# Windowed attention and a gated feed-forward layer on one core: the start of the kernel in another order

## The chip, the cores and the metric

The kernel runs on one core of a Trainium2 chip. The core has five engines with instruction streams of their own: TensorE (PE, matrix products; its weight loads are shown as PEld), VectorE (DVE), ScalarE (ACT), GpSimd (POOL) and SyncE (SP, here used only to issue DMAs). TensorE writes to PSUM (banks of 128 partitions x 512 f32); the other data lie in SBUF. DMAs can be issued by SP, ACT and POOL. Engines wait for one another by semaphores. The metric is the time of one execution on the device in microseconds (us), as a median over runs.

## The reference

Attention over 4 batches, 8 heads, 768 positions, 64 values per head, in which each position sees the first 4 positions (the sinks) and the last 128; its output, as 3072 tokens of 512 values, goes through a layer of 2048 hidden values with a gate. Cut to its core:

```python
keep = is_sink | in_window                  # pos < 4, or 0 <= row - col < 128
scores = where(keep, q @ k.T / 8, -1e9)
a = softmax(scores); x = a @ v              # all heads side by side: (3072, 512)
h = x @ w_in                                # (3072, 2048)
g = h / (1 + exp(-beta * h))
out = g @ w_out                             # (3072, 512) float32
```

All inputs are float32; the kernel works in bf16 with f32 sums.

## The kernel before, in words

**Tiles and units.** The tokens are cut into 8 tiles of 384. The attention of a tile is 4 units; a unit n is one batch, one pair of heads and one half of the sequence, 32 units in all. Units 0 to 3 give tile 0 (first halves of batch 0), units 4 to 7 tile 1 (second halves), and so on.

**What a unit does.** Its q, k and v are loaded in f32 (`load`), cast to bf16 on GpSimd (`cast`), q and k are turned on TensorE by six 128x128 transposes into one PSUM bank and copied to SBUF as `qkT` (`transpose_in`, L489 and L496; later units are turned by DMA). `scores` makes k times q for the blocks that the window touches, in two chunks (a into `s_ps`, b into `h_ps` or `s_ps`), and ScalarE takes the exponential E of each (L543). `attend` multiplies E by v with a column of ones added (`v_aug`), so that the sums come with it; for a second half the sinks come in by a product of `E_sink` and `v_sink` (L612). `normalise` divides (L632, L634), `transpose_out` turns the result and puts it in `xT`.

**Masks.** Units from ADDED = 4 on multiply E by a mask of zeros and ones on VectorE (`mask`, L554). Units below ADDED add a large negative number before the exponential: a product of the identity and `far_a` or `far_b` opens the PSUM sum (L528), 384 columns for each of two heads and two chunks.

**Sinks.** `k_sink` holds the four sink keys of a pair (L501, with the select `own_head`); `v_sink` holds the sinks' rows of v for all 16 pairs, bf16, with columns of ones. Two DMAs issued by GpSimd (L760) load and cast those rows straight into it, after VectorE has filled it with zeros.

**The feed-forward part.** For each tile and each of 16 pieces of 128 hidden values (`hidden`): four products (L671), a tanh on ScalarE (L679), the gate on VectorE (L693); `project` multiplies by w_out (L700), and the result goes out by DMA. The hidden pieces of tile 0 use two banks, `acc0` and `acc1`. The weights come in 16 pieces of 512 KB, cast on GpSimd (L456).

**Order.** The work is written down in program order, and a planner (`Prog.order`) lays it out on each engine: at each step it takes, by its own costs (`busy`, `lag`, `give`, constants for DMAs), the piece that can start first. The order on each engine is fixed in the program. Loads on SP keep their written order (`line`). `keep_busy` writes products of ones by ones into `acc1`; their results are not used, and 7 of the 21 read `k16` of unit 0 so as to stand behind its cast.

The names that the change touches: `constants` (L369), `load` (L416), `cast` (L459), `transpose_in` (L482), `scores_sink` (L507), `scores` (L521), `mask` (L545), and the opening of the program, L720 to L778.

Of the kernel before, what the change touches and what calls it, by code (L numbers as in the profile page):

```python
# [48 lines left out]
ADDED, FAR = 4, -float(1 << 20)  # L49
# [22 lines left out]
class Prog:  # L72
# [13 lines left out]
    FIRST_DMA = 1300.0  # L86
    DEPTH = 7
    LANDED, TURNED = 2000.0, 4000.0
# [70 lines left out]
    def order(self):  # L159
# [29 lines left out]
        while len(placed) < len(self.nodes):  # L189
            found = [(*b, e) for e in self.ENGINES if (b := best(e)) is not None]  # L190
            start, n, e = min(found, key=lambda f: (f[0], f[1].id))
            free[e] = start + n.busy
            if n.dma is None:
                n.done = start + n.busy + n.lag
            else:

                begin = max(dma_free[e], start + n.busy)
                others = [o for o in self.ENGINES if o != e and dma_free[o] > begin]
                dma_free[e] = begin + n.lag * (1 + len(others))
                for o in others:  # L200
                    dma_free[o] += min(n.lag, dma_free[o] - begin)
                n.done = dma_free[e] + (self.TURNED if n.dma[0][0] in "tx" else self.LANDED)
# [75 lines left out]
def bass_streamingllm_window__then__act_swish_beta_kernel(  # L278
# [50 lines left out]
    v_sink = sb("v_sink", (128, NPAIR, 2, D1), BF16)  # L329
# [32 lines left out]
    def select(out_ap, in_ap, patt, cmp, fill, base, cm, r, w):  # L362
        op("gp", lambda e: e.affine_select(out_ap, in_ap, patt, cmp, fill, base=base,
                                           channel_multiplier=cm), r=r, w=w)

    def fill(eng, ap, value, w, r=()):
        op(eng, lambda e: e.memset(ap, value), r=r, w=w)  # L367

    def constants():  # L369
# [4 lines left out]
        fill("dve", ones[:, :], 1.0, ["ones"])  # L374
# [3 lines left out]
        for z in range(4):  # L378
            fill("dve", v_aug[z][:, :, :, D:D1], 1.0, [("v_aug", z, 0), ("v_aug", z, 1)])
            fill("gp", k_sink[z][:, :], 0.0, [("k_sink", z)])  # L380
        fill("dve", v_sink[:, :, :, :], 0.0, ["v_sink"])
        fill("dve", v_sink[0:NSINK, :, 0, D:D1], 1.0, ["v_sink"], ["v_sink"])
        fill("dve", v_sink[HEAD1:HEAD1 + NSINK, :, 1, D:D1], 1.0, ["v_sink"], ["v_sink"])
# [4 lines left out]
               ["mask_b0"])  # L388
        select(two[:, :, 128:256], one, [[0, 2], [-1, 128]], ALU.is_ge, 0.0, -1, 1, ["ones"],
               ["mask_b1"])  # L390

        select(mask_a[:, 0:256], mask_b[:, 0:256], [[0, 256]], ALU.is_ge, 1.0, -NSINK, 1,
               ["mask_b0", "mask_b1"], ["mask_a"])
        select(mask_a[:, 256:TT], ones[:, 0:128], [[0, 128]], ALU.is_ge, 0.0, NSINK - 1, -1,
               ["ones"], ["mask_a1"])

        for far, m, w, names in ((far_a, mask_a, "far_a", MASK_A), (far_b, mask_b, "far_b", MASK_B)):
            op("dve", lambda e, far=far, m=m: e.tensor_scalar(far[:, :], m[:, :], -FAR, FAR, ALU.mult,
                                                              ALU.add), r=names, w=[w], **dve(300.0))
# [17 lines left out]
    def load(n, v_queue="sp"):  # L417
        b, hp, half, pb = place(n)
        t0 = half * TT
        if n < XBAR:  # L420
            for name, src in (("q", q), ("k", k)):
                s = src[b, 2 * hp:2 * hp + 2, t0:t0 + TT, :].rearrange("h (p c) d -> p h (c d)", c=3)
                d = stage[name][pb][:, :, 3 * half:3 * half + 3, :].rearrange("p h c d -> p h (c d)")
                op("sp", lambda e, d=d, s=s: e.dma_start(d, s),
                   w=[(name + "_stage", pb, half, 0), (name + "_stage", pb, half, 1)],
                   dma=f"{name}{pb}_{half}", line=True, **transfer(2 * TT * D * 4, 300))
        for name, src in (("q", q), ("k", k), ("v", v)):
            if name != "v" and n < XBAR:
                continue
            for hh in range(2):  # L430
                s = src[b, 2 * hp + hh, t0:t0 + TT, :].rearrange("(c p) d -> p c d", p=128)
                op(v_queue, lambda e, hh=hh, s=s, name=name: e.dma_start(
                    stage[name][pb][:, hh, 3 * half:3 * half + 3, :], s),
                   w=[(name + "_stage", pb, half, hh)], dma=f"{name}{pb}_{half}{hh}",
                   line=v_queue == "sp", **transfer(TT * D * 4, 230))
# [23 lines left out]
    def cast(n):  # L459
# [6 lines left out]
        for x, name in enumerate("qk"):  # L466
            op("gp", lambda e, x=x, name=name: e.tensor_copy(qk16[z][:, x, :, :, :], view(name)),  # L467
               r=[(name + "_stage", pb, half, hh) for hh in range(2)], w=[(name + "16", z)],
               busy=451.0, lag=100.0)
# [3 lines left out]
        if n >= XBAR:  # L473
            op("sp", lambda e: e.dma_start_transpose(
                qkT[pb][:, half, :, :].rearrange("p w (c x) -> p (w c) x", c=3),
                qk16[z][:, :, :, :, :].rearrange("p w c h d -> p (w c h d)")),
               r=[("q16", z), ("k16", z)], w=[("qkT", pb, half)], dma=f"t{pb}{half}",
               **transfer(2 * TT * 256, 240, 1400.0))


    def transpose_in(n, bank=tr_ps, name_of="tr", eng="dve"):
        _, _, half, pb = place(n)  # L482
        bank16 = bank[:, :].bitcast(BF16)
        z = n % NQK
        for which, name in enumerate("qk"):
            with P.together("pe"):
                for c in range(3):
                    at = (3 * which + c) * 128
                    op("pe", lambda e, which=which, c=c, at=at: nc.tensor.transpose(  # L489
                        bank16[:, at:at + 128],  # L490
                        qk16[z][:, which, c, :, :].rearrange("p h d -> p (h d)"), ident[:, :]),
                       r=[(name + "16", z), "ident"], w=[name_of], **pe(128))

        dst = qkT[pb][:, half, :, :].rearrange("x w (p c) -> x w p c", c=3)
        src = bank16[:, 0:2 * TT].rearrange("x (w c p) -> x w p c", w=2, c=3)
        op(eng, lambda e: (e.copy if eng == "act" else e.tensor_copy)(dst, src),  # L496
           x=[name_of], w=[("qkT", pb, half)], **(act(768) if eng == "act" else dve(865.0)))
# [9 lines left out]
    def scores_sink(n, bank, name):  # L507
# [3 lines left out]
           r=[("k_sink", pb), ("qkT", pb, 1)], w=[f"{name}0"], **pe(TT))  # L511
# [7 lines left out]
    def scores(n, c, bank, name):  # L519
# [11 lines left out]
        with P.together("pe"):  # L531
            for kb, qb, nq in CHUNKS[half][c]:
                w = 128 * nq
                for hh in range(2):
# [5 lines left out]
                       r=[("qkT", pb, half), ("qkT", pb, kb // 3)], w=[f"{name}{hh}"],  # L540
# [6 lines left out]
    def mask(n, c):  # L547
        if n < ADDED:
# [8 lines left out]
           r=[("E", n % 2, c), *names], w=[("E", n % 2, c)], **dve(466.0))  # L557

    def scores_at_once(n):
# [8 lines left out]
        with P.together("pe"):  # L568
            for x, kb, qb, nq in pieces:
                for hh in range(2):  # L570
# [6 lines left out]
                       r=[("qkT", pb, half), ("qkT", pb, kb // 3)], w=[("s0", "s1", "tr", "av")[bank]],  # L577
# [143 lines left out]
    for n in range(4):  # L721
        load(n, "act" if n < 2 else "sp")
    op("act", lambda e: e.dma_start(beta_stage[:, :], moe_beta.rearrange("(m p) -> m p", p=128)),
       w=["beta_stage"], dma="beta")
    load_w(0)
# [11 lines left out]
    cast(0)  # L737
    cast(1)

    def keep_busy(count, busy, behind=()):  # L740

        for _ in range(count):
            op("pe", lambda e: e.matmul(acc[1][:, 0:256], ones[:, 0:128], ones[:, :], start=True,  # L743
                                        stop=True), r=["ones", *behind], w=["acc1"], busy=busy,
               lag=260.0, give=200.0)
# [4 lines left out]
    def enter(n):  # L750
        transpose_in(n, *((tr_ps, "tr") if n % 2 == 0 else (acc[0], "acc0")), "dve")
        if n + 2 < 6:
            cast(n + 2)
        if n == 1:
            for i in range(4):
                cast_w(i)
            for hh in range(2):
                rows = slice(HEAD1 * hh, HEAD1 * hh + NSINK)
                s = v[:, :, 0:NSINK, :].rearrange("b (g h) s d -> s h (b g) d", h=2)[:, hh]
                op("gp", lambda e, hh=hh, rows=rows, s=s: e.dma_start(v_sink[rows, :, hh, 0:D], s),  # L760
                   w=[("v_sink", hh)], r=["v_sink"], dma=f"s{hh}")

    for n in range(4):
        enter(n)
        if n == 2:
            for hh in range(2):
                select(own_head[:, hh, :], ones[:, 0:NSINK], [[0, NSINK]], ALU.is_ge, 0.0, 63 - 127 * hh,
                       2 * hh - 1, ["ones"], ["own_head"])
        if n == 0:
            keep_busy(7, 200.0, [("k16", 0)])  # L770
# [18 lines left out]
    for n in range(4):  # L789
        sink_keys(n)  # L790
# [132 lines left out]
```

## Time and profile before

| what | us |
|---|---|
| median of 3 runs | 232.91 (232.72 to 233.29) |
| the profiled execution | 232.34 |
| its span | 230.6 |
| busy: PE, DVE, ACT, POOL | 219.8, 135.3, 138.7, 75.3 |
| first exponential starts | 10.05 |

The page divides the span into 40 slices of 5.77 us and gives the busy share in tenths. A row of the order of time has start, length, engine, line, operation, output and inputs, count, and in brackets the idle time before it with what ended it. In the chain of waits each piece is work that the end of the execution hung on. A transfer's time to landing counts from its issue. The granted clock in the windows is 1.00 throughout, though the early products take longer than the later ones of the same shape.

### The profile page before, as it was taken

What the parts mean: (1) busy time and instruction counts of PE and PEld (TensorE: products, weight loads), DVE (VectorE), ACT (ScalarE), POOL (GpSimd) and SP (SyncE); (2) the same over time, 40 slices, a digit from 0 to 9 for tenths busy, and PEclk for the clock granted to TensorE, in tenths of its full rate; (3) what the DMA queues carried; (4) which work ended last, traced back from release to release, by engine and by line L of the source; (5) the groups of instructions that cost most, each with busy time, mean ns of one, the idle gap of its engine ahead of it and who ended that gap; (6) DMA issues with size and microseconds to landing.
All of it is one profiled execution on the core that took longest, in us unless ns stands there. A gap on an engine that the chain in (4) does not pass through costs nothing.

```text
span 230.6 us, 4381 instructions
## 1 busy us (share of the span) xinstructions
PE 219.8 (95%) x1714; PEld 119.1 (52%) x1714; DVE 135.3 (59%) x261; ACT 138.7 (60%) x217; POOL 75.3 (33%) x152
## 2 busy tenths in 40 slices
PE   4997989899999999999999999999999999999994
PEld 2654545555455555545555555555555555555441
DVE  5364999699654654544577676566656554344300
ACT  2275886597418676645777776756766764555421
POOL 7769985797440331541202342500000000000000
PEclk9999999999999999999999999999999999999999
DMA  6999999996699996984999897631101101111012
GB/s 154 317 386 288 329 339 257 382 330 158 147 220 288 179 260 149 223 219 113 238 240 186 189 235 186 155 73 55 55 20 63 63 20 63 45 48 45 33 58 91
DMA packets 95700, 39.76 MB, mean 172 GB/s; under 512 B 82352, under 2 KB 88512, under 8 KB 95680
## 3 DMA queue, kind: packets, MB, share of 16 engines
q1 hardware_dynamic: 93504, 39.07, 64.6%
q10 hardware_dynamic: 1632, 0.40, 0.8%
q8 instruction: 13, 0.21, 0.3%
q0 software_dynamic: 544, 0.02, 0.2%
q14 instruction: 7, 0.06, 0.1%
HBM read 27.30 MB, written 6.29 MB: 146 GB/s over the span
## 4 chain that ended last, share of the span: by engine, by line
PE 84%; DVE 10%; ACT 4%; issue 1%; ACTq 0%
PE acc L700 35%; PE h_ps L671 28%; PE s_ps L623 5%; PE s_ps L573 4%; DVE g L693 4%; PE acc L671 3%; DVE E L554 3%; ACT E L543 2%; PE h_ps L700 2%; DVE qkT L496 2%; PE acc L743 1%; PE s_ps L536 1%; ACT th L679 1%; PE s_ps L489 1%; PE s_ps L612 1%; DVE v_sink L367 1%
## 5 line engine op out<-in xcount | busy, mean ns | idle before, releaser
L700 PE MATMUL acc<-w_out,g 128*128 128x512 bf16 x368 | 99.0, 380 | 0.0
L679 ACT ACTIVATE th<-h_ps,beta_half 128x384 f32<-128x384 f32 x104 | 59.5, 582 | 45.9 <-PE h_ps L671 43.8
L671 PE MATMUL h_ps<-xT,w_in 128*128 128x384 bf16 x416 | 80.7, 326 | 0.0
L693 DVE SCALAR_TENSOR_TENSOR g<-th,h_ps 128x384 bf16<-128x384 f32 x104 | 56.4, 551 | 38.2 <-ACT th L679 36.8
L671 PEld LDWEIGHTS h_ps<-xT,w_in 128*128 128x128 bf16 x416 | 39.9, 98 | 32.6 <-DVE g L693 1.4
L700 PEld LDWEIGHTS acc<-w_out,g 128*128 128x128 bf16 x368 | 33.8, 98 | 31.7 <-issue 3.0
L589 DVE TENSOR_TENSOR E<-E,mask_all 128x1536 bf16<-128x1536 bf16 x20 | 19.5, 975 | 20.2 <-ACT E L580 20.2
L580 ACT ACTIVATE E<-s_ps 128x1536 bf16<-128x1536 f32 x20 | 28.9, 1445 | 2.0 <-PE s_ps L573 1.9
L470 POOL CAST v_aug<-v_stage 128x384 bf16<-128x384 f32 x32 | 16.6, 527 | 28.1 <-DMA v_stage<-in_v_dram 14.9
L467 POOL CAST qk<-q_stage 128x384 bf16<-128x384 f32 x32 | 18.0, 562 | 23.7 <-DMA q_stage<-in_q_dram 10.8
L467 POOL CAST qk<-k_stage 128x384 bf16<-128x384 f32 x32 | 17.1, 535 | 15.2 <-DMA k_stage<-in_k_dram 13.8
L708 ACT ACTIVATE out_sb<-acc 128x512 f32<-128x512 f32 x23 | 13.6, 597 | 14.1 <-PE acc L700 13.7
L671 PE MATMUL acc<-xT,w_in 128*128 128x384 bf16 x96 | 19.0, 327 | 2.4 <-DVE g L693 1.8
L543 ACT ACTIVATE E<-s_ps 128x768 bf16<-128x768 f32 x16 | 13.0, 811 | 13.5 <-PE s_ps L536 13.5
L623 PEld LDWEIGHTS s_ps<-v_aug,E 128*128 128x128 bf16 x384 | 17.1, 97 | 5.5 <-ACT E L543 0.7
L623 PE MATMUL s_ps<-v_aug,E 128*128 128x65 bf16 x384 | 19.4, 193 | 0.5 <-ACT E L543 0.4
L634 DVE TENSOR_TENSOR o_norm<-s_ps,rden 128x384 bf16<-128x384 f32 x32 | 17.8, 557 | 1.5
L679 ACT ACTIVATE th<-acc,beta_half 128x384 f32<-128x384 f32 x24 | 13.7, 581 | 5.9 <-PE acc L671 5.2
L693 DVE SCALAR_TENSOR_TENSOR g<-th,acc 128x384 bf16<-128x384 f32 x24 | 12.8, 545 | 3.8 <-ACT th L679 3.7
L496 DVE COPY qkT<-s_ps 128x768 bf16<-128x768 bf16 x10 | 9.5, 954 | 5.5 <-PE s_ps L489 5.4
L671 PEld LDWEIGHTS acc<-xT,w_in 128*128 128x128 bf16 x96 | 8.2, 98 | 8.3 <-DVE g L693 3.2
L573 PE MATMUL s_ps<-qkT 64*128 64x256 bf16 (+2 forms) x144 | 10.1, 254 | 0.0
(65 smaller groups left out, 148.4 us busy)
## 6 DMA issues: line engine op xcount, KB each, us to landing
out_dram<-out_sb SPq DMA_DIRECT2D x24, 256.0 KB, 2.3
wst<-in_moe_w_in_dram SPq DMA_DIRECT2D x8, 512.0 KB, 5.3
wst<-in_moe_w_out_dram SPq DMA_DIRECT2D x8, 512.0 KB, 8.9
q_stage<-in_q_dram SPq DMA_DIRECT2D x8, 384.0 KB, 4.3
k_stage<-in_k_dram SPq DMA_DIRECT2D x8, 384.0 KB, 4.2
v_stage<-in_v_dram SPq DMA_DIRECT2D x8, 384.0 KB, 3.9
v_stage<-in_v_dram SPq DMA_DIRECT2D x28, 96.0 KB, 4.8
q_stage<-in_q_dram SPq DMA_DIRECT2D x12, 192.0 KB, 5.3
```

Of the source, the lines that this page charges most:

```text
L467: op("gp", lambda e, x=x, name=name: e.tensor_copy(qk16[z][:, x, :, :, :], view(name)), r=[(name + "_stage", pb, half, hh) for hh in range ...
L470: op("gp", lambda e: e.tensor_copy(v_aug[pb][:, 3 * half:3 * half + 3, :, 0:D], view("v")), r=[("v_stage", pb, half, hh) for hh in range(2 ...
L543: op("act", lambda e: e.activation(E[n % 2][:, c, :, 0:at], bank[:, 0:2, 0:at], AF.Exp, bias=0.0, scale=SCALE), x=[f"{name}0", f"{name}1"] ...
L573: op("pe", lambda e, kb=kb, bank=bank, qb=qb, at=at, nq=nq, rows=rows: e.matmul(s_ps[:, bank, 128 * at:128 * (at + nq)], qkT[pb][rows, kb ...
L580: op("act", lambda e: e.activation(E[z][:, :, :, :].rearrange("p c h x -> p c (h x)"), s_ps[:, :, :].rearrange("p (h b) x -> p h (b x)", h ...
L589: op("dve", lambda e: e.tensor_tensor(both, both, mask_all[:, half, :].unsqueeze(1).to_broadcast([128, 2, 768]), ALU.mult), r=[("E", z, 0) ...
L623: last=(x == len(kbs) - 1): e.matmul(av_ps[:, at + hh * D1:at + hh * D1 + D1], E[z][:, c, h2, col:col + 128], v_aug[pb][:, kb, hh, :], sta ...
L634: op("dve", lambda e: e.tensor_tensor(o_norm[o][:, :, :, :].rearrange("p m h d -> p (m h) d"), src[:, :, 0:D], rden[z][:, :].unsqueeze(2). ...
L671: return op("pe", lambda e: e.matmul(bank, w_in16[:, c, m * 128:(m + 1) * 128], xT[:, c, T * TT:(T + 1) * TT], start=(c == 0), stop=(c == 3)),
L679: op("act", lambda e: e.activation(th[i % 3][:, :], bank, AF.Tanh, bias=0.0, scale=beta_half[:, m:m + 1]), x=[name], r=["beta"], w=[("th", ...
L693: op("dve", lambda e: e.scalar_tensor_tensor(g[T % 2][:, m, :], th[i % 3][:, :], 1.0, bank, ALU.add, ALU.mult), r=[("th", i % 3)], x=[name ...
L700: node = op("pe", lambda e: e.matmul(bank, g[T % 2][:, m, t * 128:(t + 1) * 128], w_out16[:, m, :], start=(m == 0), stop=(m == NM - 1)), r ...
```

## The change

1. *Loads.* Of units 0 and 1, q goes by SP and k by ScalarE's queue, and of v one head by each, behind q and k of both units. Before, q and k went by SP and v by ScalarE. From unit 2 on the loads stand as before.
2. *Casts of unit 0.* k is cast on VectorE, q on GpSimd.
3. *Transposes of unit 0.* q goes into `s_ps`, copied by VectorE, k into `acc0`, copied by ScalarE. The readiness of q's half (`qT`) and of all (`qkT`) is told apart.
4. *Sinks.* `own_head` moves to `sink_constants` with the fills of `k_sink` and `v_sink`; `v_sink` is filled as 1040 f32 in place of 2080 bf16 values. The sinks' rows of v go by two plain f32 DMAs on ScalarE's queue into a part of `g[1]` (not in use yet), and VectorE casts them into `v_sink` in two copies.
5. *Masks.* ADDED is 6, so units 4 and 5 get their masks by products on TensorE.
6. *Keep-busy products.* 14, then 3 behind the transposes of unit 0, then 2 behind the attention of each of units 0, 1 and 2; none reads a cast.
7. *Order.* The transposes of unit n + 1 are written ahead of unit n's attention; `sink_keys` of units 0 to 3 stands behind the attention of unit 3; several of the planner's costs have other values.

```diff
-ADDED, FAR = 4, -float(1 << 20)
+ADDED, FAR = 6, -float(1 << 20)
...
-    FIRST_DMA = 1300.0
+    FIRST_DMA = 0.0
...
+    def sink_constants():
+        for z in range(4):
+            fill("gp", k_sink[z][:, :], 0.0, [("k_sink", z)], busy=150.0)
+        for hh in range(2):
+            select(own_head[:, hh, :], ones[:, 0:NSINK], [[0, NSINK]], ALU.is_ge, 0.0, 63 - 127 * hh,
+                   2 * hh - 1, ["ones"], ["own_head"], 150.0)
+        fill("dve", v_sink_all[:, :].bitcast(F32), 0.0, ["v_sink"], busy=1000.0)
...
-    def cast(n):
+    def cast(n, first=False):
...
+            eng = "dve" if first and name == "k" else "gp"
...
-    def transpose_in(n, bank=tr_ps, name_of="tr", eng="dve"):
+    def transpose_in(n, bank=tr_ps, name_of="tr", eng="dve", apart=None):
...
+        if apart is None:
+            copy(eng, 0, 2, bank, name_of, [("qT", pb, half), ("qkT", pb, half)])
+        else:
+            copy(eng, 0, 1, bank, name_of, [("qT", pb, half)])
+            copy(apart[2], 1, 2, apart[0], apart[1], [("qkT", pb, half)])
...
-    for n in range(4):
-        load(n, "act" if n < 2 else "sp")
+    for n in range(2):
+        load_qk(n, "q")
+        load_qk(n, "k", "act")
+    for n in range(2):
+        load_head(n, "v", 0)
+        load_head(n, "v", 1, "act")
+    load(2)
+    load(3)
...
+        op("act", lambda e, rows=rows, s=s: e.dma_start(v_rows[rows], s), w=[("v_rows", hh)],
+           dma=f"s{hh}", **transfer(1 << 14, 100))
...
+        op("dve", lambda e, hh=hh, rows=rows: e.tensor_copy(v_sink[rows, :, hh, 0:D], v_rows[rows]),
+           r=[("v_rows", hh), "v_sink"], w=[("v_sink", hh), *wide], give=3000.0, **dve(600.0))
...
-                op("gp", lambda e, hh=hh, rows=rows, s=s: e.dma_start(v_sink[rows, :, hh, 0:D], s),
-                   w=[("v_sink", hh)], r=["v_sink"], dma=f"s{hh}")
...
+    turned = enter(0)
+    keep_busy(3, 200.0, turned)
     for n in range(4):
-        enter(n)
...
-        if n == 0:
-            keep_busy(7, 200.0, [("k16", 0)])
         scores(n, 0, s_ps, "s")
         scores(n, 1, h_ps, "h")
         mask(n, 0)
         mask(n, 1)
-        attend(n)
+        if n < 3:
+            enter(n + 1)
+        ended = attend(n)
         normalise(n)
         if n < 3:
             transpose_out(n, acc[1], "acc1", "act")
+            keep_busy(2, 200.0, ended)
...
-        sink_keys(n)
+        sink_keys(n, ended)
```

More of the change, by code (lines that the diff above doesn't have):

```diff
@@ L201, in order @@
                     dma_free[o] += min(n.lag, dma_free[o] - begin)
-                n.done = dma_free[e] + (self.TURNED if n.dma[0][0] in "tx" else self.LANDED)
+                n.done = dma_free[e] + (self.TURNED if n.dma[0][0] in "tx" else
+                                        self.LANDED if start > 3000.0 else self.FIRST_LANDED)
                 landing[e].append(n.done)
@@ L373, in constants @@
            r=["ones32"], w=["scratch"])
-        fill("dve", ones[:, :], 1.0, ["ones"])
+        fill("dve", ones[:, :], 1.0, ["ones"], busy=270.0)
         select(ident[:, :], ones[:, 0:128], [[1, 128]], ALU.is_equal, 0.0, 0, -1, ["ones"], ["ident"])
@@ L378, in constants @@
         for z in range(4):
[L379 to L383, printed above, removed]
+            fill("dve", v_aug[z][:, :, :, D:D1], 1.0, [("v_aug", z, 0), ("v_aug", z, 1)], busy=60.0)
         two = mask_b[:, :].rearrange("p (r x) -> p r x", r=2)
@@ L415, in load_whole, with load_qk @@
            dma=f"{name}{pb}_00", line=True, after=after, **transfer(4 * TT * D * 4, 217, 600.0))
-    def load(n, v_queue="sp"):
+    def load_qk(n, name, queue="sp"):
         b, hp, half, pb = place(n)
[L419 to L427, printed above, removed]
-            if name != "v" and n < XBAR:
[L429 to L435, printed above, removed]
@@ L539, in scores @@
                         stop=True, skip_group_check=n < ADDED),
[L540 removed]
+                       r=[("qT", pb, half), ("qkT", pb, kb // 3)], w=[f"{name}{hh}"],
                        busy=50.0 + w / 4.8, lag=260.0)
@@ L736, in bass_streamingllm_window__then__act_swish_beta_kernel, with keep_busy @@
     load_w(7)
-    cast(0)
+    cast(0, True)
     cast(1)
-    def keep_busy(count, busy, behind=()):
+    sink_constants()
+    for hh in range(2):
+        rows = slice(HEAD1 * hh, HEAD1 * hh + NSINK)
+        op("dve", lambda e, hh=hh, rows=rows: e.tensor_copy(v_sink[rows, :, hh, 0:D], v_rows[rows]),
+           r=[("v_rows", hh), "v_sink"], w=[("v_sink", hh), *wide], give=3000.0, **dve(600.0))
+    def keep_busy(count, busy, after=None):
         for _ in range(count):
             op("pe", lambda e: e.matmul(acc[1][:, 0:256], ones[:, 0:128], ones[:, :], start=True,
-                                        stop=True), r=["ones", *behind], w=["acc1"], busy=busy,
-               lag=260.0, give=200.0)
+                                        stop=True), r=["ones"], w=["acc1"], busy=busy,
+               lag=260.0, give=200.0, after=after)
     keep_busy(14, 215.0)
     def enter(n):
-        transpose_in(n, *((tr_ps, "tr") if n % 2 == 0 else (acc[0], "acc0")), "dve")
+        if n == 0:
+            turned = transpose_in(n, tr_ps, "tr", "dve", (acc[0], "acc0", "act"))
+        else:
+            turned = transpose_in(n, *((tr_ps, "tr") if n % 2 == 0 else (acc[0], "acc0")), "dve")
         if n + 2 < 6:
@@ L756, in enter @@
                 cast_w(i)
[L757 to L760, printed above, removed]
-                   w=[("v_sink", hh)], r=["v_sink"], dma=f"s{hh}")
-    for n in range(4):
-        enter(n)
[L765 to L768, printed above, removed]
-        if n == 0:
-            keep_busy(7, 200.0, [("k16", 0)])
+        return turned
+    turned = enter(0)
+    keep_busy(3, 200.0, turned)
+    for n in range(4):
         scores(n, 0, s_ps, "s")
```

80 lines of the change are left out of this document (56 added, 24 removed).

## The prediction

> **What bounds the kernel now.** I read the page first (shares, then the 40 slices), then the chain of waits, then the order of time of the first 30 us on all engines, and last the transfers' times to landing.
>
> ```profile
> span 230.6 us, 4381 instructions
> ...
> PE   4997989899999999999999999999999999999994
> ...
> DMA  6999999996699996984999897631101101111012
> ```
>
> A slice is 5.77 us. TensorE is at 9 from the ninth slice on, so whatever ends earlier in the first eight slices should end the kernel earlier by as much. The transfers are at 6 to 9 in nearly the same slices, so the start is also a race with the DMA. In order of time, the first unit's way to its first exponential (E), the later E, and unit 3's copy before the first hidden products:
>
> ```profile
> 0.81 0.45 SPq L424 DMA_DIRECT2D q_stage<-in_q_dram  x1
> ...
> 1.32 0.45 SPq L424 DMA_DIRECT2D k_stage<-in_k_dram  x1
> ...
> 1.81 2.15 DVE L367 MEMSET v_sink<- 128x2080 bf16 x3 [0.36 <-issue]
> ...
> 3.17 0.29 POOL L363 TENSOR_SCALAR_AFFINE_SELECT mask_a<-ones 128x128 bf16<-128x128 bf16 x1
> ...
> 4.21 0.25 DVE L398 TENSOR_SCALAR far_a<-mask_a 128x384 bf16<-128x384 bf16 x1
> 4.28 1.43 POOL L760 DMA_DIRECT2D v_sink<-in_v_dram  x2 [0.82 <-DVE v_sink L367]
> ...
> 6.00 0.50 POOL L467 CAST qk<-q_stage 128x384 bf16<-128x384 f32 x1
> ...
> 6.90 0.50 POOL L467 CAST qk<-k_stage 128x384 bf16<-128x384 f32 x1
> ...
> 7.74 0.85 PE L489 MATMUL s_ps<-ident,qk 128*128 128x128 bf16 x6
> ...
> 8.62 0.96 DVE L496 COPY qkT<-s_ps 128x768 bf16<-128x768 bf16 x1 [4.16 <-PE s_ps L489]
> ...
> 10.05 0.81 ACT L543 ACTIVATE E<-s_ps 128x768 bf16<-128x768 f32 x1 [7.24 <-PE s_ps L536]
> ...
> 13.23 0.96 DVE L496 COPY qkT<-s_ps 128x768 bf16<-128x768 bf16 x1
> ...
> 13.93 0.51 POOL L467 CAST qk<-k_stage 128x384 bf16<-128x384 f32 x1 [1.31 <-PE acc L743]
> ...
> 14.63 0.81 ACT L543 ACTIVATE E<-s_ps 128x768 bf16<-128x768 f32 x1 [0.16 <-PE s_ps L536]
> ...
> 17.00 0.81 ACT L543 ACTIVATE E<-s_ps 128x768 bf16<-128x768 f32 x1 [0.48 <-PE s_ps L536]
> ```
>
> GpSimd is free of masks at 3.46 but issues the sinks' two DMAs until 5.71, because these wait for VectorE's v_sink fill; only at 6.00 does it cast unit 0's q. When that had landed:
>
> ```profile
> L424 SPq DMA_DIRECT2D q_stage<-in_q_dram x1: 452/452/452, 0.8 to 0.8; - x1
> ...
> DMA to landing us min/median/max: 3.0/3.0/3.0
> L424 SPq DMA_DIRECT2D k_stage<-in_k_dram x1: 450/450/450, 1.3 to 1.3; - x1
> ...
> DMA to landing us min/median/max: 3.2/3.2/3.2
> ```
>
> q at 3.8, k at 4.5: both lay in SBUF for over 2 us. Behind unit 3, the chain of waits goes on so:
>
> ```profile
> 20.27 0.49 ACT xT L655
> 20.76 0.05 issue
> 20.81 0.35 PE acc L671
> ...
> 25.32 0.72 DVE E L554
> ...
> 26.50 0.78 DVE E L554
> ...
> 27.75 0.76 DVE E L554
> ```
>
> Hidden products of tile 0 close at 20.81. From about 24 to 38 the chain lies mostly on VectorE, and three of the four mask multiplies of units 4 and 5 are pieces of it, 2.26 us together.
>
> **The change part by part.**
>
> *Unit 0.* GpSimd loses the 1.43 us of DMA issue and the 0.82 us wait in front. It takes one of the two own_head selects ahead and can cast q at the landing, 3.8 to 4.1 (k now starts at 0.81 on ScalarE's queue beside q, where k started 0.51 later). The k cast goes to VectorE: between far_a's 0.25 and GpSimd's 0.50, I take 0.4. VectorE must be free: the v_sink fill writes 1040 f32 in place of 2080 bf16; between the 2.15 unchanged and half of it, I take half, so far_b and far_a end near 3.8 rather than 4.46. Both casts are then done by 4.7. Transposes run at the early rate, six in 0.85 with the last one's latency, to 5.5. The copy of 768 columns in 0.96 becomes two of 384, one on VectorE (half of 0.96) and one on ScalarE (0.49 by the xT piece), in two banks: done by 6.0. Before, copy end to first E was 0.47 (9.58 to 10.05). So first E at about 6.4, a gain of 3.6.
>
> *Units 1 to 3.* All four transfers of units 0 and 1's q and k go ahead of v, so unit 1 is fed by about 5.5. The period of a unit, 14.63 to 17.00, is 2.4 us, made of two E, products and a normalisation; it stays. New on VectorE are two v_sink casts (1024 elements on 4 partitions), queued before the copies of unit 2 and unit 3, and they wait for their DMAs. By far_a's rate one costs 0.66, by the copy's 1.28; I take 1.0 as the source is f32. The DMAs replace GpSimd's cast DMAs and are issued last on ScalarE's queue, at about 3.5 to 4.4; the transfer ahead of them there was beta, whose time was
>
> ```profile
> L723 ACTq DMA_DIRECT2D beta_stage<-in_moe_beta_dram x1: 505/505/505, 3.0 to 3.0; - x1
> ...
> DMA to landing us min/median/max: 5.4/5.4/5.4
> ```
>
> so they land by about 9.8. VectorE gets there at about 9.3. The first costs 0.5 of wait and 1.0 of cast before unit 2's copy, which so starts at about 10.8 where it started at 13.23. Behind that wait stand unit 2's copy, rden and o_norm; E of unit 2 waits for them. Of the 3.6, some 0.7 goes there. GpSimd's 1.31 wait at 13.93 (keep-busy products that read unit 0's k) goes; what is late next there is unit 3's q and k, which have to land by 12. Unit 3's first E comes at about 14.1 for 17.00, its xT copy at 17.4 for 20.27, hidden products close at 17.9 for 20.81: a gain of 2.9. Transposes stand now between the scores and attention of the unit before, which only moves them. The added keep-busy products are issued into waits; without that cover two cost about 0.2.
>
> *Units 4 and 5.* Four multiplies leave VectorE (2.26 on the chain). Eight products of 384 columns come to TensorE. The same product of units 0 to 3 gives their price:
>
> ```profile
> 10.92 0.50 PE L528 MATMUL s_ps<-far_a,ident 128*128 128x384 bf16 x2 [0.25 <-ACT E L543]
> ...
> 11.25 0.33 PE L489 MATMUL s_ps<-ident,qk 128*128 128x128 bf16 x3
> ```
>
> Two hold it for 0.33, eight for 1.3; the cover is TensorE's waiting in the same stretch, seen in the windows:
>
> ```profile
> 14.00:16.00 2.00, 2.00 (x30) 1.17 (x26) 1.33 (x4) 1.84 (x3) 2.00 (x4) 1.00 1.04 391
> ...
> 20.00:22.00 2.00, 1.07 (x11) 0.59 (x10) 0.20 (x1) 1.30 (x3) 2.00 (x6) 1.00 1.01 255
> ```
>
> (window, length, busy of PE, PEld, DVE, ACT, POOL, clock, DMA share, GB/s). At most the 1.3 shows, at least nothing.
>
> *The DMA's wall.* The order of SP's queue from unit 2 on is untouched, so later landings hold still.
>
> ```profile
> k_stage<-in_k_dram SPq DMA_DIRECT2D x1, 192.0 KB, 7.5
> ```
>
> (size, and us from issue to landing) and in order of time
>
> ```profile
> 10.93 0.57 SPq L424 DMA_DIRECT2D k_stage<-in_k_dram  x1
> ...
> 22.84 1.04 POOL L456 CAST w_in<-wst 128x1024 bf16<-128x1024 f32 x1 [0.33 <-DMA wst<-in_moe_w_in_dram]
> ...
> 25.63 0.77 POOL L467 CAST qk<-k_stage 128x384 bf16<-128x384 f32 x1
> ...
> 28.57 0.50 PE L489 MATMUL s_ps<-ident,qk 128*128 128x128 bf16 x6
> ```
>
> Unit 4's k lands at 18.4. The w_in piece at 22.84 and unit 6's k at 25.63 follow their landings, so they stay; unit 6's transposes began at 28.57, 2.2 after that cast ended (26.40). That is the slack: up to there about 2.2 can be gained, whatever the front and the masks give.
>
> *Sum.* Front 2.9, masks 2.26 off, products up to 1.3 on: 2.9 + 2.3 - 1.3 = 3.9 if the DMA lets it, 2.2 by the wall at unit 6. I take 2.3, as the wall holds one unit and a little comes back from casts that no longer run beside a mask multiply (0.77 for 0.50). From tile 1 on the same work is left. The profiled execution took 232.34, its span 230.6, so 1.74 lie around it; new span 228.3, execution 230.0. The median of the runs stands 0.57 above the profiled one (232.91), so 230.6.
>
> **The rivals.** *More comes through* (3.9): the wall passes over unit 6 because its place in TensorE's order is behind other ready work. For it: 2.26 on VectorE's chain. Time 229.0. Against: unit 6 is also in the chain of the first tile, whose products have two banks.
>
> *The transfers take it all:* DMA at 9 and waits for w_in; if the transfers of units 4 to 6 come later by more k ahead of v, the 2.2 of slack shrinks to about 0.4. Against: the bytes ahead of unit 4 are the same. Time 232.5.
>
> *Slower, by TensorE's clock.* Early products run at half rate:
>
> ```profile
> 5.81 2.13 PE acc L743 x10
> ```
>
> 0.213 for 256 columns, where the 384 at 10.92 take 0.165, that is 0.11 for 256. If the new order, with waits between a few products from 5 to 14, does not reach the fast rate before unit 3, each unit pays for it: TensorE is busy 2.00 of 2.00 at 14 to 16, some of it latency, so I take half of the period, 1.2, for three units: 3.6 more, 234.2. It decides from two slow units on (2.4 against the gain of 2.3). Against it: the window at 20 to 22 has only 1.07 us of busy TensorE, and the products behind it run at the full rate (28.57: six transposes in 0.50, which took 0.85 at 7.74), so short waits alone do not bring the slow rate back. I give it 0.09. The Trainium skill's page "TensorE: Matmul & The Clock Gate" (Part 1: The HAM clock gate) states that the array starts at half rate, is released after about 3.4 us of sustained work and falls back after an idle window of that length; its Part 4 (PE-mode transpose) adds that transposes do not count as busy in the same way. Read strictly, that speaks against a start with few plain products, and the time by it would be this rival's, where by the rows it is the likeliest one's.
>
> **How the numbers follow.** Likeliest, 230.6: 0.66. More, 229.0: 0.13. Transfers, 232.5: 0.12, of which 0.10 within what a measurement of this kernel tells from no change, about 0.3% or 0.7 us. Slower: 0.09. So faster 0.66 + 0.13 + 0.02 = 0.81, same 0.10, slower 0.09. The likeliest one's own range is 229.6 to 231.8 (casts of 0.66 to 1.28, and none to 1.3 of the products). The range for 8 in 10 takes in the second and most of the third: 228.8 to 233.0, with the slower case left out.
>
> **What would show it.** Right: unit 0's first E near 6.4, unit 3's near 14, the close of the first hidden products near 17.9, VectorE's L554 multiplies of units 4 and 5 gone, unit 6's transposes near 26.4, tile 1 earlier by about 2.3 and the last slices alike. Wrong: VectorE idle before a v_sink cast until past 11; half-rate products past 10; unit 6's k cast later than 25.7; or the gain at 18 there but given back by 40, which would say that the first tile is bound by something else than VectorE.

## The result and the profile after

| | before | changed |
|---|---|---|
| median of 5 runs, us | 232.91 (232.72 to 233.37) | 229.99 (229.84 to 230.45) |
| the profiled execution, its span | 232.34, 230.6 | 230.45, 228.7 |

The ratio is 0.9873, with a 95% interval of 0.9857 to 0.9889: 2.9 us faster, 0.6 below the forecast of 230.6. The profiled execution of the changed kernel is the slowest of its five, 0.46 above their median; a second one, in the experiments below, took 229.70 with a span of 228.0. All ratios here are of undisturbed executions: seven of the twelve of one run below, the kernel before with half of w_in, took 5 to 6 us longer at a lower clock and are left out.

The page of the changed kernel, the span and the slices of TensorE and of the DMA:

```profile
span 228.7 us, 4395 instructions
...
PE   7988988999999999999999999999999999999994
...
DMA  6999999998689999996999998601101201111112
```

From the eighth slice on TensorE is at 9 (before, from the ninth on), and the last slices are alike. What has gone lies in the slices ahead of that. The changed kernel in order of time, unit 0's way to its first E, the two new casts, then unit 3's E and its copy (columns as before):

```profile
3.93 0.50 POOL L481 CAST qk<-q_stage 128x384 bf16<-128x384 f32 x1 [0.25 <-DMA q_stage<-in_q_dram]
4.13 0.55 DVE L481 CAST qk<-k_stage 128x384 bf16<-128x384 f32 x1 [0.49 <-DMA k_stage<-in_k_dram]
...
5.04 0.53 PE L504 MATMUL acc<-ident,qk 128*128 128x128 bf16 x3
5.28 0.56 DVE L513 COPY qkT<-s_ps 128x384 bf16<-128x384 bf16 x1 [0.60 <-PE s_ps L504]
...
6.68 0.81 ACT L567 ACTIVATE E<-s_ps 128x768 bf16<-128x768 f32 x1 [0.60 <-PE s_ps L560]
6.89 0.51 PE L504 MATMUL acc<-ident,qk 128*128 128x128 bf16 x6
...
9.43 0.76 DVE L780 CAST v_sink<-g 4x1024 bf16<-4x1024 f32 x1
...
11.87 0.69 DVE L780 CAST v_sink<-g 4x1024 bf16<-4x1024 f32 x1
...
14.30 0.81 ACT L567 ACTIVATE E<-s_ps 128x768 bf16<-128x768 f32 x1 [0.77 <-PE s_ps L560]
...
17.58 0.48 ACT L679 COPY xT<-s_ps 128x384 bf16<-128x384 bf16 x1 [0.26 <-PE s_ps L675]
```

q and k of unit 0 are cast at their landing (3.93 and 4.13 in place of 6.00 and 6.90), and the first E starts at 6.68 for 10.05. The v_sink casts have no idle time in front, so nothing waited for the sinks' rows. Unit 3's first E comes 2.70 earlier. Then, on GpSimd and TensorE, the entry of unit 4 and of unit 6:

```profile
18.25 1.04 POOL L469 CAST w_in<-wst 128x1024 bf16<-128x1024 f32 x1 [1.58 <-DMA wst<-in_moe_w_in_dram]
...
19.22 0.51 POOL L481 CAST qk<-q_stage 128x384 bf16<-128x384 f32 x1
...
19.79 0.34 PE L504 MATMUL s_ps<-ident,qk 128*128 128x128 bf16 x3 [0.47 <-POOL qk L481]
...
26.18 0.51 POOL L481 CAST qk<-k_stage 128x384 bf16<-128x384 f32 x1
...
26.93 0.33 PE L504 MATMUL s_ps<-ident,qk 128*128 128x128 bf16 x3
```

GpSimd idles 1.58 for a piece of w_in. Unit 4's casts stand behind that piece, and TensorE waits 0.47 for the cast of its q, which ends at 19.73. Before, unit 4's six transposes began at 21.14, behind the hidden products that close at 20.81; the gain of 2.70 at unit 3's E is 1.35 at unit 4's transposes. The wait is less than what is lost; the other part is worked out below.

### The profile page after: what moved, and what is told of

The parts are those of the page before. It is cut to its first block, busy times and chain, and to the rows that moved or that the text cites. A ratio compares the mean times of both kernels' runs of the same rounds, so it can differ in the third digit from the quotient of the medians.

```text
span 228.7 us, 4395 instructions
## 1 busy us (share of the span) xinstructions
PE 220.6 (96%) x1724; PEld 119.5 (52%) x1724; DVE 134.6 (59%) x260; ACT 139.1 (61%) x218; POOL 73.3 (32%) x149
## 4 chain that ended last, share of the span: by engine, by line
PE 85%; DVE 4%; DMA 4%; SPq 4%; ACT 1%; POOL 1%; issue 1%; ACTq 0%
PE acc L724 36%; PE h_ps L695 30%; PE acc L695 4%; PE s_ps L647 4%; PE s_ps L597 4%; DMA wst<-in_moe_w_in_dram 4%; SPq L438 2%; PE h_ps L724 2%; PE s_ps L504 1%; DVE E L578 1%; DVE g L717 1%; SPq L430 1%; PE s_ps L560 1%; PE s_ps L636 1%; PE s_ps L533 1%; DVE qkT L513 1%
## 5 line engine op out<-in xcount | busy, mean ns | idle before, releaser
L481 POOL CAST qk<-q_stage 128x384 bf16<-128x384 f32 x32 | 17.3, 542 | 24.8 <-DMA q_stage<-in_q_dram 10.3
L481 POOL CAST qk<-k_stage 128x384 bf16<-128x384 f32 x31 | 16.1, 521 | 16.1 <-DMA k_stage<-in_k_dram 16.1
L513 DVE COPY qkT<-s_ps 128x768 bf16<-128x768 bf16 (+1 forms) x10 | 9.1, 914 | 1.8 <-PE s_ps L504 1.8
```

What stands on the lines that cost most here:

```text
L481: op(eng, lambda e, x=x, name=name: e.tensor_copy(qk16[z][:, x, :, :, :], view(name)), r=[(name + "_stage", pb, half, hh) for hh in range( ...
```

## The experiments

Each comparison has the kernel before beside it on the same chip (medians 232.57, 232.45 and 232.56 in three groups). Marks of the profiled executions, in us from the start of the span; "T4" is the first of unit 4's transposes on TensorE, "w_in cast" the start of that on GpSimd just ahead of unit 4's casts (no entry where three such casts run on end), "last xT copy" the start of the copy that the last products of hidden pieces 0 and 1 need:

| kernel | first E | unit 3's E | last xT copy | w_in cast | T4 | span | span - T4 |
|---|---|---|---|---|---|---|---|
| before | 10.05 | 17.00 | 20.27 | | 21.14 | 230.6 | 209.5 |
| changed, first profile | 6.68 | 14.30 | 17.58 | 18.25 | 19.79 | 228.7 | 208.9 |
| changed again (x1) | 6.13 | 13.75 | 17.02 | 17.43 | 18.97 | 228.0 | 209.0 |
| masks back (x2) | 6.37 | 13.98 | 17.26 | 16.87 | 18.83 | 228.0 | 209.2 |
| masks only (x5) | 10.02 | 16.97 | 20.24 | | 21.11 | 229.9 | 208.8 |
| sinks by GpSimd (x6) | 6.22 | 14.05 | 17.32 | 18.03 | 19.57 | 228.2 | 208.6 |
| changed, half of w_in (x8) | 6.04 | 14.96 | 18.23 | 16.02 | 19.81 | 228.4 | 208.6 |
| one bank in unit 0 (x9) | 6.78 | 14.41 | 17.82 | 16.71 | 18.76 | 227.9 | 209.1 |
| no products between (x10) | 6.08 | 13.74 | 17.40 | 16.84 | 18.39 | 227.5 | 209.1 |

From unit 3's E to the last copy of tile 0's xT it takes 3.27 or 3.28 before and in the changed kernel, so what is lost of the front's gain is lost between this copy and T4: 0.87 before, 2.21 and 1.95 in the two profiles of the changed kernel, 1.57 with the masks back. The rows of the kernel before, then those of x2:

```profile
18.85 1.14 PE L671 MATMUL acc<-xT,w_in 128*128 128x384 bf16 x6
...
20.81 0.50 PE L671 MATMUL acc<-xT,w_in 128*128 128x384 bf16 x2 [0.57 <-ACT xT L655]
...
21.14 0.50 PE L489 MATMUL s_ps<-ident,qk 128*128 128x128 bf16 x6
```

```profile
16.87 1.04 POOL L469 CAST w_in<-wst 128x1024 bf16<-128x1024 f32 x1 [0.65 <-DMA wst<-in_moe_w_in_dram]
...
17.79 0.10 PEld L695 LDWEIGHTS acc<-xT,w_in 128*128 128x128 bf16 x1 [0.47 <-ACT xT L679]
17.85 0.51 POOL L481 CAST qk<-q_stage 128x384 bf16<-128x384 f32 x1
...
17.96 0.38 PE L786 MATMUL acc<-ones 128*128 128x256 bf16 x2
...
18.18 0.81 PE L695 MATMUL acc<-xT,w_in 128*128 128x384 bf16 x4
...
18.83 0.33 PE L504 MATMUL s_ps<-ident,qk 128*128 128x128 bf16 x3
```

In both, the eight products of hidden pieces 0 and 1 stand ahead of T4. Before, six of them come ahead of the last xT copy and two wait for it. In the changed kernel and in x2 three come ahead, and five wait, with two keep-busy products among them (17.96): three products of 0.165 and two of 0.11 more, 0.7. In x2 and x8 this is the whole loss, for there the cast of unit 4's q ends before TensorE gets to T4 (18.36 against 18.83 in x2). In the two profiles of the changed kernel the late cast adds 0.64 and 0.38 (0.47 and 0.21 of idle time in the rows, which count the last product's latency as busy). In x9 and x10 six products come ahead again, and from the copy to T4 it takes 0.94 and 0.99, though the copy itself comes 0.1 and 0.4 later behind unit 3's E. This is read off the rows; no run changes that order alone.

**The masks: the changed kernel again, with them back, and alone on the kernel before.** The second and third have one edit:

```diff
-ADDED, FAR = 6, -float(1 << 20)
+ADDED, FAR = 4, -float(1 << 20)
```

> The changed kernel once more, for a second profile beside the other runs. The first profile puts the close of the first hidden products 2.7 us earlier than before (18.1 for 20.8), but hidden piece 14 only 0.5 us earlier (40.2 for 40.7), and the first products with w_out 2.1 us earlier (53.8 for 55.8). Theory T (the prediction's: front and masks give it, the order of the tail is neutral) expects 230.0 within 0.3 and, if the late transfers of the first profile are one execution's chance, piece 14 near 38.5. Theory R (the gain of the front is lost by 40 us in every execution, and the rest comes from the tail's other order) expects the same 230.0, with piece 14 again at 40 to 40.4.

> The changed kernel with the masks of units 4 and 5 back on VectorE (ADDED = 4); the order on the engines is the changed kernel's but for these instructions. Theory T: VectorE gets 2.3 us of its chain back and TensorE loses 1.3 us of products, the DMA's wall takes part of the difference, so 230.5 to 231.3, 231.0 likeliest. The rival, that the first tile is bound by transfers alone, expects 230.0 within 0.3.

> The kernel before with the masks of units 4 and 5 on TensorE (ADDED = 6), nothing else written differently. The prediction's sum gives 2.3 us off VectorE's chain and up to 1.3 on TensorE, so 1.0 faster than before, 231.6 to 231.9. The rival, after the run with the masks put back cost nothing: 0 within 0.5, because what the multiplies hold up waits for transfers or for TensorE anyway.

Measured: the changed kernel again 230.09 (ratio 0.9903, interval 0.9877 to 0.9929), masks back 230.06 (0.9900, 0.9874 to 0.9926), masks alone on the kernel before (ADDED 6 for 4) 231.73 (0.9964, 0.9952 to 0.9977). So the masks give 0.7 alone and nothing that can be measured on top of the new start; by span minus T4 it is 0.7 and 0.2. The expectation for the repeat took the hidden piece at 40.18 in the first profile for the wrong counterpart: counted through, it is piece 15, which the kernel before ran at 42.02, so 1.8 of the gain were still there at 40 us. The theory that the gain was lost by then (R) came from that miscount. Masks back lies below the 230.5 to 231.3 that was expected, within its rival's range.

**The order of the rest.** The changed kernel with every engine's order of the kernel before from hidden piece 14 on, and the reverse:

```diff
+CUT = 317
...
         placed = self.order()
+        rank = {lab: x for x, lab in enumerate(TAIL)}
+        placed[CUT:] = sorted(placed[CUT:], key=lambda n: rank["%d%s%d" % (n.lab[0], n.lab[1][0], n.lab[2])])
```

> The changed kernel up to hidden piece 14, and from there the order on every engine of the kernel before (same instructions, same waits by data). Theory T: 230.0 within 0.3, the order of the tail is neutral. Theory R: what the first profile shows between 40 and 54 us, 1.6 us of the gain (2.1 less 0.5), goes, 231.3 to 231.9.

> The kernel before up to hidden piece 14, and from there the order on every engine of the changed kernel. Theory T: 232.9 within 0.3. Theory R: 1.0 to 1.6 us faster than before, 231.3 to 231.9.

Measured: 230.54 (0.9922, 0.9898 to 0.9947) and 231.94 (0.9981, 0.9962 to 0.9999). Both point the same way, 0.45 lost and 0.6 gained with the planner's new order of the rest, but the first interval overlaps that of the changed kernel and the second just misses 1. About 0.5, not settled.

**The sinks' rows back on GpSimd,** as two casting DMAs straight into v_sink:

```diff
-        op("act", lambda e, rows=rows, s=s: e.dma_start(v_rows[rows], s), w=[("v_rows", hh)],
-           dma=f"s{hh}", **transfer(1 << 14, 100))
...
-        op("dve", lambda e, hh=hh, rows=rows: e.tensor_copy(v_sink[rows, :, hh, 0:D], v_rows[rows]),
-           r=[("v_rows", hh), "v_sink"], w=[("v_sink", hh), *wide], give=3000.0, **dve(600.0))
...
+                op("gp", lambda e, hh=hh, rows=rows, s=s: e.dma_start(v_sink[rows, :, hh, 0:D], s),
+                   w=[("v_sink", hh)], r=["v_sink"], dma=f"s{hh}")
```

> The changed kernel with the sinks' rows of v fetched again by GpSimd's two casting DMAs straight into v_sink, and without the two plain DMAs and VectorE's two casts. Theory T: the planner puts these DMAs behind the casts of unit 2 or 3 or before unit 0's; 1.4 us of GpSimd come back somewhere in the first 12 us. If ahead of unit 0's cast: first E 1.4 to 2 us later and the time 231.0 to 232.0. If behind the first units' casts: little is lost and the 1.4 us of VectorE's casts are won, 229.6 to 230.4.

Measured: 229.99 (0.9896, 0.9876 to 0.9915). In order of time:

```profile
3.93 0.50 POOL L481 CAST qk<-q_stage 128x384 bf16<-128x384 f32 x1 [0.22 <-DMA q_stage<-in_q_dram]
...
4.53 1.44 POOL L794 DMA_DIRECT2D v_sink<-in_v_dram  x2
...
6.22 0.81 ACT L567 ACTIVATE E<-s_ps 128x768 bf16<-128x768 f32 x1 [0.44 <-PE s_ps L560]
...
14.05 0.81 ACT L567 ACTIVATE E<-s_ps 128x768 bf16<-128x768 f32 x1 [0.76 <-PE s_ps L560]
```

The issue still costs GpSimd 1.44, now behind unit 0's q cast, and the first E keeps its place. So the gain of unit 0 came from what stands ahead of its cast, not from taking the DMAs away from GpSimd. Without the two casts on VectorE it still takes 7.83 from the first E to unit 3's (7.62 with them, 6.95 before): they aren't what stretches the front.

**The transfers.** Both kernels with half of each w_in piece loaded, and that half cast twice, so the hidden values are others than the reference's:

```diff
         view, src, _ = w_piece(i)
+        if i < NW:
+            view, src = view[:, :, 0:256], src[:, :, 0:256]
```

> The kernel before with half of each w_in piece loaded (256 of 512 columns, cast twice; the hidden values of the other columns are wrong), so 2 MB fewer in the first 31 us at the same instructions on all engines. Theory T (the transfers bind the first tile only once the front is early): 232.6 to 232.9, at most 0.3 faster, since before GpSimd waited 0.3 to 0.5 us at each of four pieces. Rival (transfers bind both): 1 us or more faster.

> The changed kernel with half of each w_in piece loaded in the same way (the hidden values of the other columns are wrong). Theory T: the DMA's wall took part of the 3.2 us of the front and all that the masks gave; without it the changed kernel gains 0.8 to 1.6 us more, 228.5 to 229.3. Rival (the first tile is bound by its two banks and the engines, not by transfers): 230.0 within 0.3.

Measured: the kernel before 0.9973 (0.995 to 0.9996), about 0.6 less, between the two expectations (at most 0.3, or 1 and more), so that it decides neither; the changed one 229.86 (0.9892, 0.987 to 0.9913), as with all of w_in. Its order of time, and that of the changed kernel again below it:

```profile
9.13 0.72 DVE L785 CAST v_sink<-g 4x1024 bf16<-4x1024 f32 x1
9.25 0.96 POOL L486 CAST qk<-k_stage 128x384 bf16<-128x384 f32 x1
...
11.97 2.48 POOL L474 CAST w_in<-wst 128x1024 bf16<-128x1024 f32 x2
...
12.33 1.22 DVE L785 CAST v_sink<-g 4x1024 bf16<-4x1024 f32 x1
...
17.00 0.51 POOL L486 CAST qk<-q_stage 128x384 bf16<-128x384 f32 x1
...
19.81 0.33 PE L509 MATMUL s_ps<-ident,qk 128*128 128x128 bf16 x3
...
22.80 0.51 POOL L486 CAST qk<-k_stage 128x384 bf16<-128x384 f32 x1
...
23.30 0.81 PE L700 MATMUL acc<-xT,w_in 128*128 128x384 bf16 x4
...
27.35 0.33 PE L509 MATMUL s_ps<-ident,qk 128*128 128x128 bf16 x3
```

```profile
17.43 1.04 POOL L469 CAST w_in<-wst 128x1024 bf16<-128x1024 f32 x1 [1.19 <-DMA wst<-in_moe_w_in_dram]
...
18.41 0.51 POOL L481 CAST qk<-q_stage 128x384 bf16<-128x384 f32 x1
...
18.97 0.34 PE L504 MATMUL s_ps<-ident,qk 128*128 128x128 bf16 x3 [0.21 <-POOL qk L481]
...
22.09 0.81 PE L695 MATMUL acc<-xT,w_in 128*128 128x384 bf16 x4
...
25.16 0.51 POOL L481 CAST qk<-k_stage 128x384 bf16<-128x384 f32 x1
...
26.14 0.33 PE L504 MATMUL s_ps<-ident,qk 128*128 128x128 bf16 x3
```

Two readings. At unit 6 the transfers do not bind: its k is cast 2.4 earlier with half of w_in, yet its transposes follow hidden piece 4 by 4.05 in both (23.30 to 27.35, 22.09 to 26.14). At unit 4 they do in the full kernel (the cast of q ends at 18.92, and TensorE follows at once) and not in the other one, where TensorE comes 2.3 after that cast has ended. That this did not show in the time goes with the same rows: GpSimd's casts ran beside VectorE's v_sink casts, both took longer (1.22 for 0.67 in x1, 0.96 for 0.51, two w_in casts in 2.48 for 2.03), and unit 3's E came 1.2 later. That these are all of the 1.2 is not shown. The median alone would have said that the transfers don't matter; the test took one wait away and put other delays in its place.

**Unit 0 in one bank,** k cast on GpSimd, one copy of 768 columns; tail order held:

```diff
-    cast(0, True)
+    cast(0)
...
-            turned = transpose_in(n, tr_ps, "tr", "dve", (acc[0], "acc0", "act"))
+            turned = transpose_in(n, tr_ps, "tr", "dve")
```

> The changed kernel with unit 0 as before in one respect: k cast on GpSimd behind q, all six transposes in one bank, one copy of 768 columns on VectorE. From hidden piece 14 on every engine's order is the changed kernel's. The prediction's steps: the k cast ends some 0.3 later, the copy 0.46 later (0.96 for 0.50), so unit 0's first E some 0.8 later (6.9 to 7.3); the units' period is untouched, so unit 3's first E and the end move as much: 230.8. Rival: the front's end is set by the cast of w_in that follows its landing at 17.4, and the 0.8 vanishes: 230.0 within 0.3.

Measured: 230.16 (0.9897, 0.9869 to 0.9924), so no loss. In order of time:

```profile
6.78 0.81 ACT L646 ACTIVATE E<-s_ps 128x768 bf16<-128x768 f32 x1 [3.95 <-PE s_ps L639]
...
8.45 0.81 ACT L646 ACTIVATE E<-s_ps 128x768 bf16<-128x768 f32 x1 [0.16 <-PE s_ps L639]
...
14.41 0.81 ACT L646 ACTIVATE E<-s_ps 128x768 bf16<-128x768 f32 x1 [0.49 <-PE s_ps L639]
...
18.20 0.51 POOL L560 CAST qk<-q_stage 128x384 bf16<-128x384 f32 x1 [0.45 <-DMA q_stage<-in_q_dram]
...
18.35 0.50 PE L774 MATMUL acc<-xT,w_in 128*128 128x384 bf16 x2 [0.57 <-ACT xT L758]
...
18.76 0.34 PE L583 MATMUL s_ps<-ident,qk 128*128 128x128 bf16 x3
```

The first E is 0.65 later, near the 0.8 expected. Unit 1's is where it was (8.46 in x1), but the planner has a part in that: in x1 unit 1's scores stand on TensorE behind unit 0's attention and start at 8.08, here they stand ahead of it and start at 8.07. Unit 3's E is 0.66 later again, and T4 is 0.21 earlier. Two things end together there: the cast of unit 4's q, which waited for its landing, at 18.71, and the last two hidden products, which wait for xT, at 18.68 (18.35 and twice 0.165). T4 can be early because only two hidden products stand behind the xT copy here; in x1 there are five. So the rival has the time right, but the cast of w_in that it names isn't what T4 waits for here, and as the edit brought another order on TensorE with it, the run doesn't show what the split would be worth at the end by itself.

**No keep-busy products between the units:**

```diff
-    keep_busy(3, 200.0, turned)
...
-            keep_busy(2, 200.0, ended)
```

> The changed kernel without the seven added keep-busy products that stand between the units' transposes and their first hidden products (the three behind unit 0's transposes stay, taken from the fourteen at the start); tail order as in the changed kernel. The prediction's step (they are issued into waits and cost nothing, and short waits don't bring the slow rate back): 230.0, or up to 0.3 less; six transposes stay at about 0.5. Rival, TensorE's clock: without them the products of units 1 to 3 fall back to half rate (384 columns x2 in 0.6 and more where they take 0.33), and the time is 231 to 234.

The edit takes out nine products (three, and two behind each of three units), not seven; the fourteen of the start are left.

Measured: 229.29 (229.01 to 230.16; 0.9874, 0.9842 to 0.9907), the lowest of all and below both expectations, 0.6 and 0.9 below ADDED 8 and the one-bank kernel of the same group; the ranges overlap. Three transposes among the attention of unit 2, and the first hidden products (16.82 in x1):

```profile
11.15 0.34 PE L583 MATMUL acc<-ident,qk 128*128 128x128 bf16 x3
...
15.98 1.14 PE L774 MATMUL acc<-xT,w_in 128*128 128x384 bf16 x6
```

At 0.34 for three the full rate holds without them. Whether the 0.6 is theirs stays open. Unit 3's E is where it was, and T4 comes 0.58 earlier than in x1 by two things at once: the w_in piece was cast 0.59 earlier in this execution, and six hidden products stand ahead of the last xT copy in place of three.

**More masks on TensorE,** ADDED 8 and ADDED 12:

```diff
-ADDED, FAR = 6, -float(1 << 20)
+ADDED, FAR = 8, -float(1 << 20)
```

> The changed kernel with the masks of units 6 and 7 on TensorE as well (ADDED 8): four multiplies of 0.54 to 1.2 less on VectorE, eight products of 0.165 more on TensorE. Theory V, that VectorE back to back from 29 to 37 us binds units 6 and 7 in the changed kernel: 229.2 (0.8 less, as the masks of units 4 and 5 were worth 0.8 alone). Rival P, that TensorE is as full there: 230.0 to 230.8. The tail's order comes out another way, worth 0.5 to either side.

> The changed kernel with the masks of units 6 to 11 on TensorE (ADDED 12): beside the eight products of units 6 and 7, sixteen of 0.165 in tile 1, where TensorE is at 9 in every slice. If TensorE alone binds tile 1, the sixteen cost 2.6 over ADDED 8: 231.8 to 232.6. If VectorE holds TensorE up there, less than 231.

Measured: 229.90 (0.9889, 0.9861 to 0.9918) and 232.02 (0.9987, 0.9968 to 1.0006). The windows of ADDED 8, and below it of the changed kernel (window, length, busy of PE, PEld, DVE, ACT, POOL, clock, DMA share, GB/s):

```profile
30.00:40.00 10.00, 9.81 (x93) 5.76 (x92) 7.10 (x16) 6.91 (x12) 6.20 (x11) 1.00 1.05 307
```

```profile
30.00:40.00 10.00, 8.38 (x87) 4.93 (x85) 9.51 (x20) 6.76 (x11) 7.56 (x13) 1.00 1.04 305
```

VectorE gets 2.4 us back there and TensorE is filled, and the time stays where it was, within the noise: by these windows the bound only changes hands, as the rival said. The sixteen products in tile 1 cost 2.1 more, near the 2.6 worked out from TensorE's rate alone.

## Why the prediction was right, and where it was not

*Unit 0: right.* 3.4 and 3.9 in two executions for 3.6; the difference goes with TensorE's rate, as three transposes of unit 0 took 0.53 in the first and 0.33 in the second. The k cast took 0.55 for 0.4, the fill with two small ones 1.29 where half of 2.15 was taken, the copies 0.56 and 0.48. But the cause is narrower than the text had it: DMA issue behind the q cast costs nothing (x6), and the split over two engines and banks gives 0.65 at the first E and no more time at the end in x9, whose order is another. What is left is the cast at the landing; no run makes that cast late by itself.

*Units 1 to 3: right in size, wrong in cause.* Forecast 0.7 lost on the way and 2.9 left; measured 0.67 lost and 2.70 left (0.67 and 3.25 the second time). The v_sink casts cost 0.76 and 0.69 for 1.0 each, the wait of 0.5 for their rows did not come, and without the casts the stretch is no shorter (x6). In the rows of x1, unit 1's scores come behind unit 0's attention on TensorE; in x9 they come ahead of it and the stretch is 7.63 (7.62 in x1) all the same, so that is not the cause by itself. From unit 2's E to unit 3's it takes 2.65 in both and 2.37 before: in that stretch TensorE's scores of a unit now wait for VectorE's reciprocal of the unit before (0.32 at 13.37 in x1), where they stood ahead of it (16.62 and 16.68). That is read off, not tested.

*Units 4 and 5: the mis-sized term.* 2.26 off VectorE against at most 1.3 on TensorE was a net 1.0 to 2.3. It gave 0.7 alone and 0.0 on top of the new start (0.2 by span minus T4).

*The DMA's wall: right number, wrong place.* The cap of 2.2 at unit 6 lies within the 1.9 to 2.6 by which the span came out shorter, and unit 6's transposes began at 26.93 and 26.14 for 26.4. But it isn't what caps: with its k in 2.4 earlier they came no sooner behind piece 4. The loss comes two units ahead, at unit 4, and transfers are a part of it: GpSimd waits 1.19 to 1.58 for a piece of w_in with unit 4's casts queued behind it, and of the 1.1 to 1.35 that unit 3's gain loses there, this is 0.4 to 0.6 (nothing in x2). The other 0.7 is TensorE's own order. The prediction looked at landings that stay put, and not at what is queued behind the one that comes late; it carried the close of the hidden products over from the kernel before (17.9 for 20.81), where the product behind the xT copy now closes piece 0 alone (18.1) and piece 1 follows from 18.50 on; and it gave the added keep-busy products no time, where two of them take 0.2 of that 0.7. One of its signs of being wrong, unit 6's k cast later than 25.7, came up in the first profile (26.18) and not in the second (25.16). From T4 on the time left is 208.6 to 209.5 in all rows of the table, so the forecast of 2.3 held by some luck: two wrong sizes, masks too large and a wall too late, were cut to nearly the same sum.

*From tile 1 on the same work is left: not quite.* The work is the same, its order isn't, and that order may be worth 0.5 (x3, x4).

*The rivals.* "More comes through" at 229.0 had masks that give little. "The transfers take it all" names transfers of q and k that come later; the transfer that eats a part is a piece of w_in. "Slower, by TensorE's clock" fell, and the opposite took place: the products that ran at half rate until some time past 9 in the kernel before (three transposes in 0.53 at 8.81) ran at the full rate from 6.89 on in the first profile of the changed one (six in 0.51), and from 4.68 in the second. The Trainium skill's page "TensorE: Matmul & The Clock Gate" (Part 1: The HAM clock gate) lets the rate rise after about 3.4 us of sustained work. The second profile agrees (3.4 after the first product at 1.28); the first one, where it took about 5, does not. That a first stretch of fast products moved the later rows was not tested by itself.

## What to carry to other kernels

Follow a gain at the start to the next point where two engines meet, and ask on each what stands in its order ahead of that point: here, at unit 4's transposes, GpSimd's cast of a weight piece that landed late and TensorE's own hidden products each took a part of the gain, and from that point on all variants in the table take the same time to within 0.9 us. Work that is moved off a busy engine is worth what the next engine lets through (2.26 us of multiplies gave 0.7 or nothing), so price it in the stretch as it will be after the other parts of the change. A test that makes transfers lighter moves their consumers too; read its rows before its median.

## What the runs showed of the hardware

Some instructions of VectorE and of GpSimd took longer where they ran side by side: VectorE's mask multiplies and v_sink casts, whose operands all lie in SBUF, and GpSimd's casts. A cast beside VectorE's copy out of PSUM did not (0.51 at 21.03 in the first profile of the changed kernel, beside a copy from 20.98 to 21.94). Rows of the changed kernel again (x1), two mask multiplies, which both run beside casts, and the cast beside the second:

```profile
30.65 0.63 DVE L578 TENSOR_TENSOR E<-E,mask_b 128x768 bf16<-128x768 bf16 x1
...
32.15 0.89 DVE L578 TENSOR_TENSOR E<-E,mask_b 128x768 bf16<-128x768 bf16 x1
...
32.58 0.83 POOL L481 CAST qk<-k_stage 128x384 bf16<-128x384 f32 x1
```

The multiply took 0.55 in x8 where GpSimd was idle, 0.63 and 0.89 here, and 1.17 in the first profile beside a cast of w_in; the cast of 384 columns 0.51 alone and 0.83 to 0.97 beside such instructions; the v_sink cast 0.67 to 0.76 in the changed kernel and 1.22 beside casts of w_in. The prediction had this at one cast only (0.77 for 0.50).

Executions of one kernel differ by when a piece of w_in lands: its cast came at 18.25 and at 17.43 in two profiles of the changed kernel, and 0.82 later there is 0.82 later at T4 and 0.7 in the span. Single profiles of a start that hangs on a landing should be compared by such marks, not by their spans alone.
